# Giving two chains of small steps top priority, and moving the end's gradient and stores to other engines, in a decode backward kernel

## The chip, the core and the metric

The kernel runs on one core of a Trainium2 chip. The time is device microseconds of one launch. Thirteen runs of the kernel before gave a median of 498.91 us, from 496.43 to 502.22. The execution that was profiled took 496.43 us, and its span (first to last instruction) is 494.7 us.

## The reference

The forward pass is one decode step of a layer with two branches that run beside each other, for two sequences and one new token each. `D` is 576, there are 32 query heads on 16 key and value heads of 128, 4096 cached keys per head, and a gated layer of width 4608:

```
xn  = layernorm(x)
q   = xn @ wq                        # 32 heads of 128
p   = softmax(q k^T / sqrt(128))     # over 4096 cached keys, two query heads share a kv head
out = x + (p v) @ wo + ((xn @ w_gate) * (xn @ w_up)) @ w_down
```

What is computed is `out` and the gradient of all eight inputs for a given `grad_out`: `x`, the two caches, `wq`, `wo`, `w_gate`, `w_up`, `w_down`. Everything is bf16. The gradients of the caches are outer products (probabilities times output gradient for V, score gradients times queries for K), each as large as the cache: 92 MB are read, 92 MB written.

## The kernel before, in words

**Steps.** The 16 key and value heads are taken in 4 groups of 4. A group has 4 steps (2 sequences, and 2 heads at a time), so there are 16 steps (the loop over `n`, L887). A step loads two K heads and two V heads, 1 MB each, into a pool of 12 buffers (tag `nat`). VectorE (DVE) transposes each half head (`X`, L547, L141), and TensorE (PE) makes the scores of it (`ps_sc`, L556).

**The softmax chain** (`softmax`, L623) follows when both K heads of the step have scores. It is a row of small instructions that hand over from engine to engine: DVE copies the scores (`s_sb`, L565), PE transposes them (L569), DVE takes row maxima (`mx`, L626), PE transposes these (L628), DVE takes the maxima of 4 (`m4`, L630), PE spreads them (L632), DVE makes the bias (`negb`, L635), ScalarE (ACT) takes the exponential and its sum (`ex`, L641), PE adds the sums (L643), DVE inverts (`rz`, L645), scales (`pr`, L648) and transposes (`rowT`). **The score gradient chain** (`dscores`, L657) does the like after the V heads: L565, L569, L661, L666, L668, L669 and a transpose. Its first product needs `ex`, so it stands behind the softmax chain of the same step.

**What hangs on the chains.** GpSimd (POOL) spreads each result under a mask (`prm` and `dsm`, L597). Each of the two then feeds 8 outer product units (`outer_units`, L601): two PE matmuls of 512 columns into `ps_o`, and one eviction of 128x1024 to a store tile `so` by ACT (L124). After four units POOL issues a store of 1 MB (L618). The rows also go into `contract` (L572): 64 small matmuls with the V or K heads, which is the last use of these heads, so their buffers come free only then, and SP can issue the next loads.

**Side work.** The gated layer and the end of each group (`back_units`: output projection, gradients of `wq` and `wo`) are cut into units, which the loop mixes in (`side`, L779). They evict with ACT too.

**The end.** After the loop (L930) the list `ending` is filled. From there `evac` (L116) deals the evictions out to ACT and DVE by a running sum of costs, and every third pair of outputs goes to the banks of the scores (`ps_x`). The remaining units are mixed with the units of the last gradient, in this order: `prepare`, the first two units of the last group, `output`, `rows`, `gradient` (L854), then the stores of the last `wo` and `wq` gradients: `outer_o` (tile `sto`, L764), `outer_q` (`stq`, L730) and `outer_qt` (`stqt`, L745), all issued by POOL. `gradient` works on 2x576 numbers: two reductions on DVE (L858, L862), then five DVE instructions (L867, L869, L870, L871, L873) and a store by SP (L874).

**What sets the order.** Each engine takes its instructions strictly in its queue's order. The orders are fixed when the kernel is built: the framework walks through its own model of the run and gives an engine, among the instructions whose inputs the model holds ready, the one that stands first in the program. Inside `tc.high_priority()` an instruction counts as standing ahead of all others. `Block` (L95) has always used this for groups of matmuls that belong together. SP's queue holds all loads, POOL's queue holds the stores as well as POOL's arithmetic.

Of the kernel before, what the change touches and what calls it, by code (L numbers as in the profile page):

```python
# [9 lines left out]
ALU = mybir.AluOpType  # L10
# [3 lines left out]
P = 128  # L14


def view(t, p0, np_, off, dims):

    (pstep, _), *_ = t.ap
    return bass.AP(t.tensor, t.offset + p0 * pstep + off, [[pstep, np_], *[list(d) for d in dims]])  # L20
# [3 lines left out]
def kernel(  # L24
# [22 lines left out]
    nc = tc.nc  # L47
# [8 lines left out]
    GH = 2 * G  # L56
    NGRP = Hkv // G
# [16 lines left out]
    def ps_m(shape, dtype=FP32):  # L74
        return ps.tile(list(shape), dtype, tag="m", bufs=2, name="ps_m")
# [4 lines left out]
    def ps_o():  # L80
        return ps.tile([P, 2, 512], FP32, tag="o", bufs=2, name="ps_o")
# [52 lines left out]
    def dve(us):  # L134
        load["v"] += us
# [59 lines left out]
    xn_f = sb.tile([2, D], FP32, tag="nat", bufs=12, name="xn_f")  # L195
# [6 lines left out]
    rstd = const.tile([2, 1], FP32, name="rstd")  # L202
# [74 lines left out]
    def tailtile(name):  # L277
        return sb.tile([P, FS], BF16, tag="stt", bufs=2, name=name)
# [399 lines left out]
    def back_units(st):  # L678
        g, wq, wo, oT = st["g"], st["wq"], st["wo"], st["oT"]
        n0 = g * GH * Dh  # L680
        m = {}
        stq = nat if g == NGRP - 1 else swtile

        def first():
            yp = ps_m([P, 5, 2])
            with Block() as mm:
                for dc in range(5):
                    for h in range(GH):
                        mm(yp[:, dc, :], lhsT=wo[:, h, DOFF[dc]:DOFF[dc] + P], rhs=oT[:, 0, h, 0:2],
                                         start=(h == 0), stop=(h == GH - 1))  # L690
            nc.vector.tensor_add(acc[:], acc[:], yp[:])

            rp = ps_m([P, 2, 2, P], BF16)
            for t in range(2):
                for h in range(GH):
                    a = h // 2
                    nc.tensor.transpose(rp[32 * a:32 * a + 32, t, h % 2, :], oT[:, t, h, :], ident[:])
            m["R"] = R = sb.tile([P, 2, 2, P], BF16, tag="R", bufs=1, name="R")
            nc.vector.tensor_copy(R[:], rp[:])
            rp = ps_m([P, 32, 2])  # L700
            for be in range(4):
                nc.tensor.matmul(view(rp[:], 0, P, 2 * be, [[8, 8], [1, 2]]),
                                 lhsT=sel[:, be].rearrange("p a i -> p (a i)"), rhs=oT[:, 1, :, 0:2],
                                 start=True, stop=True)
            m["W"] = stationaries(rp[:], lambda h: (P * h, [[1, P]]))
            dve(0.2 + 0.5)

        def second():
            dxn(*m["W"], wq, lambda q, s: (s // 4) * 16 + q * 4 + s % 4, lambda s: s // 4, 2)

        def outer_q(k, A):
            def f():
                R = m["R"]
                if A == 0:
                    m["st"] = stq([P, 2, GH * P], "stq")
                st = m["st"]
                o, whole = ps_pair()
                with Block() as mm:
                    for dc in range(2):
                        for aa in range(2):  # L720
                            a = 2 * A + aa
                            d0 = (2 * k + dc) * P
                            mm(o[aa][:, 256 * dc:256 * dc + 256], lhsT=xnr[32 * a:32 * a + 32, d0:d0 + P],
                                             rhs=R[32 * a:32 * a + 32, 1].rearrange("p h d -> p (h d)"),
                                             start=True, stop=True)
                evac_pair(lambda aa: view(st[:], 0, P, 512 * A + 256 * (aa or 0),
                                          ([[256, 2]] if aa is None else []) + [[GH * P, 2], [1, 256]]), o, whole, 1024,
                          lambda x: x.rearrange("p a (d n) -> p a d n" if whole is not None else "p (d n) -> p d n", d=2))
                if A == 1:
                    nc.gpsimd.dma_start(out_4[256 * k:256 * k + 256, n0:n0 + GH * P].rearrange("(c p) n -> p c n", p=P),  # L730
                                        st[:])
            return f

        def outer_qt():
            R = m["R"]
            st = tailtile("stqt")
            for A in range(2):
                o = ps_o()
                with Block() as mm:
                    for aa in range(2):  # L740
                        a = 2 * A + aa
                        mm(o[64 * A:64 * A + 64, aa, 0:256], lhsT=xnr[32 * a:32 * a + 32, 512:576],
                                         rhs=R[32 * a:32 * a + 32, 1].rearrange("p h d -> p (h d)"), start=True, stop=True)
                evac(st[64 * A:64 * A + 64].rearrange("p (a n) -> p a n", a=2), o[64 * A:64 * A + 64, :, 0:256], 512)
                nc.gpsimd.dma_start(out_4[512:576, n0 + 512 * A:n0 + 512 * A + 512], st[64 * A:64 * A + 64])  # L745

        def outer_o(A, h2, k):
            def f():
                R = m["R"]
                if h2 == 0 and k == 0:  # L750
                    m["so"] = stq([P, 4, D], "sto")
                o, whole = ps_pair()
                with Block() as mm:
                    for aa in range(2):
                        a = 2 * A + aa
                        mm(o[aa][:, 0:HD2], lhsT=R[32 * a:32 * a + 32, 0, h2, :],
                                         rhs=dyr[32 * a:32 * a + 32, k * HD2:(k + 1) * HD2], start=True, stop=True)
                so = m["so"]
                evac_pair(lambda aa: view(so[:], 0, P, h2 * D + k * HD2 + 2 * D * (aa or 0),
                                          ([[2 * D, 2]] if aa is None else []) + [[1, HD2]]), o, whole, D,  # L760
                          lambda x: x[:, :, 0:HD2] if whole is not None else x[:, 0:HD2])
                if h2 == 1 and k == 1:
                    r0 = n0 + 4 * A * P
                    nc.gpsimd.dma_start(out_5[r0:r0 + 4 * P, :].rearrange("(h p) n -> p h n", p=P), m["so"][:])  # L764
            return f

        return [[first], [second], [outer_o(0, 0, 0), outer_o(0, 0, 1)], [outer_o(0, 1, 0), outer_o(0, 1, 1)],
                [outer_o(1, 0, 0), outer_o(1, 0, 1)], [outer_o(1, 1, 0), outer_o(1, 1, 1)],
                [outer_q(0, 0), outer_q(0, 1)], [outer_q(1, 0), outer_q(1, 1)], [outer_qt]]
# [43 lines left out]
    def final_units():  # L813
        m = {}
# [39 lines left out]
        def gradient():  # L854
            rowf, xn_f, dy_f = m["rowf"], m["xn"], m["dy"]
            dxn = rowf[:, 1, :]
            m1 = fin([2, 1], FP32, "m1")
            nc.vector.reduce_sum(m1[:], dxn, axis=AX.X)  # L858
            nc.vector.tensor_scalar(m1[:], m1[:], 1.0 / D, None, op0=ALU.mult)
            xs2 = fin([2, D], FP32, "xs2")  # L860
            m2 = fin([2, 1], FP32, "m2")
            nc.vector.tensor_tensor_reduce(  # L862
                out=xs2[:], in0=dxn, in1=xn_f[:], scale=1.0 / D, scalar=0.0,
                op0=ALU.mult, op1=ALU.add, accum_out=m2[:],
            )
            t1 = fin([2, D], FP32, "t1")
            nc.vector.tensor_scalar(t1[:], dxn, m1[:], None, op0=ALU.subtract)  # L867
            t3 = fin([2, D], FP32, "t3")
            nc.vector.tensor_scalar(t3[:], xn_f[:], m2[:], None, op0=ALU.mult)  # L869
            nc.vector.tensor_sub(t1[:], t1[:], t3[:])  # L870
            nc.vector.tensor_scalar(t1[:], t1[:], rstd[:], None, op0=ALU.mult)  # L871
            dx_bf = fin([2, D], BF16, "dx_bf")
            nc.vector.tensor_add(dx_bf[:], t1[:], dy_f[:])  # L873
            nc.sync.dma_start(out_1.rearrange("b s d -> (b s) d"), dx_bf[:])  # L874

        return [[prepare], [output], [rows], [gradient]]
# [6 lines left out]
    st = group_front(0, *loaded)  # L883
# [3 lines left out]
    for n in range(NIT):  # L887
        g, b, s = step(n)
# [7 lines left out]
        s_ps = ps_sc()  # L896
        for x in range(2):
            K.append(slot(kview, 0, b, l0 + x, s_ps, per, (lambda: end_of_K(*last[:5])) if x == 0 and last else None))
            if x == 0:
# [3 lines left out]
                        side[0:0] = back_units(last[0])  # L903
                        per = -(-len(side) // 4)
                bd1 = build_bd(st, b, s, 1)
        pr, pT, ex, rz = softmax(s_ps)
        prm = masked(pr, "prm")
        if n + 1 < NIT and not new:
            build_W(st, *step(n + 1)[1:], 0)
        dp_ps = ps_sc()  # L910
# [9 lines left out]
                    build_W(nxt, 0, 0, 0)  # L920
        if n + 1 < NIT:
            build_W(nxt if new else st, *step(n + 1)[1:], 1)
        ds, dsT = dscores(pr, ex, rz, dp_ps)
        dsm = masked(ds, "dsm")
        end_of_V(st, b, s, V, pT)
        last = (st, b, s, K, dsT, dsm, bd0)
        if new:
            st = nxt
# [40 lines left out]
```

## Time and profile before

| what | value |
|---|---|
| median of 13 runs (lowest, highest) | 498.91 us (496.43, 502.22) |
| profiled execution: its time, its span | 496.43 us, 494.7 us |
| busy: PE, PEld, DVE, ACT, POOL | 390.9, 259.2, 327.6, 348.4, 264.2 us |
| moved by DMA | 186.06 MB, 376 GB/s over the span |
| 0 to 440 us: DMA share, GB/s | 1.00, 392 |
| 440 to 494.7 us: DMA share, GB/s | 0.68, 248 |

Busy time is that of an engine's own instructions; issuing a DMA counts as busy on POOL only, where it takes 0.75 to 0.8 us for a store of 1 MB. The DMA share is the mean busy share of the core's 16 DMA engines; at 1 and 400 GB/s or more they have nothing left. The last load of a head is issued at 416.57 us and lands at 432.60; from then on only stores are left. In the timeline each row has a start, a duration, the engine, the line, what is written and read, and in brackets how long the engine had been idle and for whom it had waited.

### The profile page before, as it was taken

To read this page: it belongs to the slowest core of one execution; us is meant where nothing else is said; L and a number is where in the kernel's file an instruction comes from. 1 tells how busy PE (TensorE), PEld (TensorE's weight loads), DVE (VectorE), ACT (ScalarE), POOL (GpSimd) and SP (SyncE) were. 2 spreads that over 40 slices of the span, in tenths; PEclk is the share of its full clock that TensorE was granted. 3 is DMA by queue.
4 is the path that set the end of the run, shared out by engine and by line. 5 is a ranking of instruction groups with operands and counts; after the bars stand their busy time and mean duration, and the time that the engine had idled before them with its cause. 6 is when DMAs were issued, how large, how long until landed. Compare 5 with 4: busy or idle time off the path is not lost.

```text
span 494.7 us, 17062 instructions
## 1 busy us (share of the span) xinstructions
PE 390.9 (79%) x7417; PEld 259.2 (52%) x7417; DVE 327.6 (66%) x680; ACT 348.4 (70%) x439; POOL 264.2 (53%) x404
## 2 busy tenths in 40 slices
PE   2677979877878876889998778669888969898943
PEld 1565656654645554556665446446556537564510
DVE  6786794862839674955887475566777564984383
ACT  4143867768647957868986678748886767899833
POOL 3245456663635555576546346547647336587613
PEclk9965998899969989988999789969999798999995
DMA  7998999999999999999999999989999999996665
GB/s 250 384 399 317 354 415 399 422 419 408 339 393 362 411 416 366 419 414 411 402 419 406 418 418 347 416 366 369 407 422 408 416 422 363 414 383 239 261 260 191
DMA packets 52900, 186.06 MB, mean 376 GB/s; under 512 B 4141, under 2 KB 19129, under 8 KB 44633
## 3 DMA queue, kind: packets, MB, share of 16 engines
q1 hardware_dynamic: 28392, 92.49, 48.6%
q0 software_dynamic: 24432, 92.48, 47.2%
q8 instruction: 58, 0.95, 0.7%
q14 instruction: 18, 0.14, 0.1%
HBM read 92.48 MB, written 92.48 MB: 374 GB/s over the span
## 4 chain that ended last, share of the span: by engine, by line
PE 30%; DMA 28%; ACT 13%; DVE 9%; issue 9%; POOL 5%; POOLq 0%; ACTq 0%; DVEq 0%
DMA out_dram<-so 20%; PE ps_o L105 14%; ACT so L124 10%; PE ps_m L105 8%; PE ps_sc L105 5%; DMA kv<-in_A_k_cache_dram 4%; DVE X L141 4%; DMA out_dram<-stw 4%; POOL bd L532 2%; ACT std L124 1%; POOL prm L597 1%; DVE Xw L141 1%; PE ps_m L591 1%; POOL out_dram L764 1%; ACT stw L124 1%
## 5 line engine op out<-in xcount | busy, mean ns | idle before, releaser
L124 ACT CAST so<-ps_o 128x1024 bf16<-128x1024 f32 x249 | 238.6, 1022 | 68.8 <-PE ps_o L105 52.8
L141 DVE STREAM_TRANSPOSE X<-kv 128x1024 f32<-128x1024 f32 x128 | 157.3, 1232 | 34.1 <-PE ps_sc L105 14.1
L105 PEld LDWEIGHTS <-X 128*128 128x128 bf16 x2048 | 81.8, 103 | 32.3 <-DVE X L141 15.5
L105 PE MATMUL ps_sc<-W,X 128*128 128x64 bf16 (+1 forms) x2048 | 90.4, 200 | 6.2 <-DVE X L141 5.2
L618 POOL DMA_DIRECT2D out_dram<-so x64 | 50.0, 782 | 72.1 <-ACT so L124 47.5
L105 PE MATMUL ps_o<-bd,prm 128*128 128x512 bf16 x254 | 78.5, 412 | 11.5 <-ACT so L124 5.0
L105 PE MATMUL ps_o<-bd,dsm 128*128 128x512 bf16 x250 | 80.0, 411 | 8.6 <-ACT so L124 7.1
L532 POOL TENSOR_TENSOR bd<-dense,maskq 128x1024 bf16<-128x1024 bf16 x32 | 60.6, 1892 | 12.9 <-DVE dense L529 11.6
L124 ACT CAST stw<-ps_o 128x1024 bf16<-128x1024 f32 x36 | 34.4, 1020 | 16.2 <-PE ps_o L105 9.3
L124 ACT CAST std<-ps_o 128x576 bf16<-128x576 f32 x36 | 21.1, 649 | 29.0 <-PE ps_o L105 21.5
L105 PE MATMUL ps_m<-kv,rowT 128*32 128x128 bf16 x2048 | 38.1, 230 | 4.2 <-issue 4.0
L514 POOL COPY W<-rep 32x16 bf16<-32x16 bf16 x128 | 25.0, 195 | 26.7 <-PE ps_sc L105 18.9
L105 PEld LDWEIGHTS <-prm 128*128 128x128 bf16 x256 | 21.8, 104 | 30.5 <-issue 17.7
L597 POOL TENSOR_TENSOR prm<-pr,maskc 128x1024 bf16<-128x1024 bf16 x16 | 30.2, 1889 | 13.7 <-DVE pr L648 13.0
L105 PEld LDWEIGHTS <-dsm 128*128 128x128 bf16 x256 | 22.1, 104 | 27.8 <-issue 20.5
L105 PEld LDWEIGHTS <-rowT 128*32 128x32 bf16 x2048 | 31.8, 102 | 9.0 <-issue 7.0
L597 POOL TENSOR_TENSOR dsm<-ds,maskc 128x1024 bf16<-128x1024 bf16 x16 | 30.4, 1900 | 5.8 <-DVE ds L669 5.5
L124 ACT CAST sto<-ps_o 128x576 bf16<-128x576 f32 x27 | 16.4, 650 | 14.1 <-PE ps_o L105 12.8
L141 DVE STREAM_TRANSPOSE Xw<-wgu 128x1152 f32<-128x1152 f32 x18 | 24.2, 1354 | 2.2 <-PE ps_sc L105 2.2
L105 PEld LDWEIGHTS <-Wdy 128*128 128x128 bf16 x306 | 21.0, 104 | 7.8 <-DVE Xo L141 2.9
L414 POOL DMA_DIRECT2D out_dram<-stw x18 | 13.9, 770 | 18.0 <-ACT stw L124 18.0
L105 PEld LDWEIGHTS <-xnr 32*128 32x128 bf16 (+1 forms) x440 | 12.8, 97 | 20.0 <-issue 15.5
(186 smaller groups left out, 552.2 us busy)
## 6 DMA issues: line engine op xcount, KB each, us to landing
out_dram<-so POOLq DMA_DIRECT2D x64, 1024.0 KB, 12.8
kv<-in_A_k_cache_dram SPq DMA_DIRECT2D x32, 1024.0 KB, 13.0
kv<-in_A_v_cache_dram SPq DMA_DIRECT2D x32, 1024.0 KB, 15.6
out_dram<-stw POOLq DMA_DIRECT2D x18, 512.0 KB, 11.8
wd<-in_B_w_down_dram SPq DMA_DIRECT2D x9, 576.0 KB, 7.6
out_dram<-std POOLq DMA_DIRECT2D x9, 576.0 KB, 9.7
wo<-in_A_wo_dram SPq DMA_DIRECT2D x4, 1152.0 KB, 12.7
wgu<-in_B_w_gate_dram SPq DMA_DIRECT2D x9, 512.0 KB, 14.2
```

The source lines that it names most:

```text
L105: ins = nc.tensor.matmul(*args, **kwargs)
L124: nc.scalar.copy(out, in_)
L141: nc.vector.transpose(out, in_)
L414: nc.gpsimd.dma_start(out[0:512, f0:f0 + FS].rearrange("(c p) n -> p c n", p=P), st[:])
L514: nc.gpsimd.tensor_copy(view(W[t][:], 32 * a, 32, 48 + 4 * a, [[2 * WW, 4], [WW + 2, 2], [1, 2]]), view(st["rep"][:], 32 * a, 32, t * 4 * ...
L532: nc.gpsimd.tensor_tensor(bd[:], view(dense[:], 0, P, 0, [[Dh, 2], [0, 4], [1, Dh]]), view(maskq[:], 0, P, 0, [[0, 2], [1, 4], [0, Dh]]), ...
L591: nc.tensor.matmul(t_ps[:], lhsT=o_sb[:], rhs=RV[:].rearrange("p x r -> p (x r)"), start=True, stop=True)
L597: nc.gpsimd.tensor_tensor(m[:], view(rows[:], 0, P, 0, [[0, 8], [1, P]]), view(maskc[:], 0, P, 0, [[1, 8], [0, P]]), ALU.mult)
L618: nc.gpsimd.dma_start(oview[b, :, :, l0 + x].rearrange("a m n -> m a n"), st[:].rearrange("p a c d -> p a (c d)"))
L764: nc.gpsimd.dma_start(out_5[r0:r0 + 4 * P, :].rearrange("(h p) n -> p h n", p=P), m["so"][:])
```

## The change

Three edits:

- `softmax` and `dscores` are traced inside `tc.high_priority()`, on every engine they use (DVE, PE, ACT). The mask products `prm` and `dsm`, the contractions and the outer products are not.
- In the last group alone (`g == NGRP - 1`) the stores of `sto`, `stq` and `stqt` are issued by SP in place of POOL.
- In `gradient` the five DVE instructions become four on POOL: both `tensor_scalar` take `rstd` as a second operand, so that the separate multiplication (L871) goes. The two reductions stay on DVE.

```
+        store = nc.sync.dma_start if g == NGRP - 1 else nc.gpsimd.dma_start
...
-                    nc.gpsimd.dma_start(out_4[256 * k:256 * k + 256, n0:n0 + GH * P].rearrange("(c p) n -> p c n", p=P),
+                    store(out_4[256 * k:256 * k + 256, n0:n0 + GH * P].rearrange("(c p) n -> p c n", p=P),
...
-                nc.gpsimd.dma_start(out_4[512:576, n0 + 512 * A:n0 + 512 * A + 512], st[64 * A:64 * A + 64])
+                store(out_4[512:576, n0 + 512 * A:n0 + 512 * A + 512], st[64 * A:64 * A + 64])
...
-                    nc.gpsimd.dma_start(out_5[r0:r0 + 4 * P, :].rearrange("(h p) n -> p h n", p=P), m["so"][:])
+                    store(out_5[r0:r0 + 4 * P, :].rearrange("(h p) n -> p h n", p=P), m["so"][:])
...
-            nc.vector.tensor_scalar(t1[:], dxn, m1[:], None, op0=ALU.subtract)
+            nc.gpsimd.tensor_scalar(t1[:], dxn, m1[:], rstd[:], op0=ALU.subtract, op1=ALU.mult)
             t3 = fin([2, D], FP32, "t3")
-            nc.vector.tensor_scalar(t3[:], xn_f[:], m2[:], None, op0=ALU.mult)
-            nc.vector.tensor_sub(t1[:], t1[:], t3[:])
-            nc.vector.tensor_scalar(t1[:], t1[:], rstd[:], None, op0=ALU.mult)
+            nc.gpsimd.tensor_scalar(t3[:], xn_f[:], m2[:], rstd[:], op0=ALU.mult, op1=ALU.mult)
+            nc.gpsimd.tensor_sub(t1[:], t1[:], t3[:])
             dx_bf = fin([2, D], BF16, "dx_bf")
-            nc.vector.tensor_add(dx_bf[:], t1[:], dy_f[:])
+            nc.gpsimd.tensor_add(dx_bf[:], t1[:], dy_f[:])
...
-        pr, pT, ex, rz = softmax(s_ps)
+        with tc.high_priority():
+            pr, pT, ex, rz = softmax(s_ps)
...
-        ds, dsT = dscores(pr, ex, rz, dp_ps)
+        with tc.high_priority():
+            ds, dsT = dscores(pr, ex, rz, dp_ps)
```

## The prediction

> **What bounds the kernel now.** I read the page first, its DMA row above all: 40 slices, a digit for the busy tenths of the 16 DMA engines.
>
> ```profile
> DMA  7998999999999999999999999989999999996665
> ```
>
> From the second slice to the 36th the DMA engines are full, so in the middle an engine that is earlier gains little; what is to be had is idle DMA time. In windows of 5 us it adds up to about 9 us before 440 us (the first load 2.7, then 45 to 55, 130 to 135, 295 to 305 and 330 to 335 us) and about 18 us after 440, where only stores are left: 13.55 MB, which at the 400 GB/s of the full stretches are 34 us of the 54.7. So the end is where I look next, cut at the places where the timeline changes character. Columns: stretch, length, busy us (count) of PE, PEld, DVE, ACT, POOL, PE clock, DMA share, GB/s.
>
> ```profile
> 448.00:455.50 7.50, 5.43 (x35) 2.27 (x36) 1.79 (x5) 7.46 (x9) 4.98 (x6) 1.00 0.60 205
> 455.50:463.50 8.00, 7.29 (x181) 4.82 (x181) 4.00 (x15) 6.91 (x9) 7.02 (x5) 1.00 0.65 247
> 463.50:473.00 9.50, 8.48 (x113) 3.61 (x111) 4.96 (x9) 8.53 (x12) 2.93 (x6) 1.00 0.85 321
> 473.00:476.10 3.10, 2.36 (x13) 0.82 (x13) 2.20 (x8) 0.00 (x0) 0.00 (x0) 1.00 0.97 361
> 478.30:481.30 3.00, 0.00 (x0) 0.00 (x0) 2.86 (x6) 0.00 (x0) 0.00 (x0) 0.97 0.85 321
> 481.30:487.70 6.40, 4.30 (x27) 1.21 (x26) 5.04 (x9) 4.13 (x6) 3.03 (x5) 0.50 0.54 191
> ```
>
> ACT evicts without a gap from 448 to 455.5, nearly so to 473, and then stands still for 3.10 us and later for 3.00 us, the second time together with PE and POOL. The end is bound by evictions first, then by the chain of the last gradient, which passes through DVE and PE ahead of the evictions queued behind it.
>
> **The priority, in the last step.** The timeline around the last softmax:
>
> ```profile
> 448.04 7.43 ACT L124 CAST so<-ps_o 128x1024 bf16<-128x1024 f32 x8 [0.24 <-PE ps_o L105]
> 448.39 0.08 DVE L635 DVE_READ_ACCUMULATOR2_ANT negb<- 128x1 f32 x1
> 455.32 0.42 ACT L641 ACTIVATE ex<-ps_sc,negb 128x128 f32<-128x128 f32 x1
> 455.85 0.29 DVE L661 CUSTOM_DVE_ANT_0 ds<-ex,ps_sc 128x128 bf16<-128x128 f32 x1 [5.91 <-ACT ex L641]
> ```
>
> The exponential's bias is there at 448.5, but it stands in ACT's queue behind eight evictions and starts at 455.3; DVE waits 5.91 us for it. At top priority it goes after the eviction that is running (7.43 / 8 = 0.93 us each), so by 449.5, and all that hangs on it comes 5 to 6 us earlier: `pr`, `prm`, both `contract` calls, the last group's units and the gradient. No work is saved on ACT (0.65 us of exponential only change places with evictions), so the gain is ACT's idle time alone. In 455.5 to 463.5 ACT is idle 1.1 us (waiting for the first `prm` units), in 463.5 to 473 it is 1.0, and in 473 to 476.1 it is 3.10: there PE waits with the `rows` matmuls (L845) for `accx`, and the evictions' matmuls stand behind them in PE's queue. With that chain 5 us earlier `accx` is there before PE asks. Bounds: nothing, if POOL's stores keep the gradient back anyway (the second `Wt` copy, L292 at 470.04, waits 2.5 us behind a store), and 5.2 us, if all three go. I take the 3.1 and a little of the rest: **3.5 us**.
>
> **The priority, in the middle.** One step shows how the order hurts there:
>
> ```profile
> 316.39 0.24 DVE L630 TENSOR_REDUCE m<-ps_m 1x4 f32<-1x128 f32 x1
> ...
> 323.82 1.25 DVE L141 STREAM_TRANSPOSE X<-kv 128x1024 f32<-128x1024 f32 x1 [7.19 <-DMA kv<-in_A_k_cache_dram]
> 324.99 0.12 DVE L635 CUSTOM_DVE_ANT_0 nb<-ps_m,R 128x4 f32<-128x4 f32 x1
> ...
> 326.25 0.64 ACT L124 CAST std<-ps_o 128x576 bf16<-128x576 f32 x1 [7.04 <-PE ps_o L105]
> ```
>
> `negb` stands behind a transpose that waits 7.19 us for a load; meanwhile ACT starves for 7.04 us. From the copy of the scores (309.7) to `pr` (329.2) this chain takes 19.5 us, in the step at 390.9 it takes 18.8, in the quickest (337.7 to 343.2) 5.5. The contractions that free the heads' buffers hang on it: the last K loads are issued at 414.08 after `pr` at 409.7. So loads are issued earlier and idle spots such as 130 to 135 and 330 to 335 us (shares 0.79 and 0.69, about 1.0 and 1.6 us lost) may fill. But the DMA engines are full elsewhere, and the first load's 2.7 us stay. Gain between nothing and some 5 us; as most spots follow loads of the gated layer too, I take **1 us**. What it may cost is the third rival.
>
> **The gradient off DVE.** Five DVE rows go, of which first, last and the store that waited:
>
> ```profile
> 478.36 0.51 DVE L867 TENSOR_SCALAR t<-rowf,m 2x576 f32<-2x576 f32 x1
> ...
> 480.65 0.75 DVE L873 TENSOR_TENSOR dx_bf<-t,dy_f 2x576 bf16<-2x576 f32 x1
> ...
> 482.99 0.75 POOL L764 DMA_DIRECT2D out_dram<-sto  x1 [4.75 <-DVE sto L121]
> ```
>
> Their durations are 0.51 + 0.50 + 0.75 + 0.51 + 0.75 = 3.0 us, 478.36 to 481.4, and this is the stretch in which PE, ACT and POOL do nothing at all: DVE's evictions of `sto` (L121, 481.33) are next in its queue, PE waits for their banks, ACT for PE, the store for all. Bounds: nothing, and 4.4 us (PE's whole wait); I take **3.0 us**, since what follows is the same work 3.0 us earlier.
>
> On POOL four instructions come in. POOL has done such work once, and the mask product is the nearest with two inputs:
>
> ```profile
> 448.04 2.30 POOL L826 TENSOR_SCALAR xn_f<-x_f,mu,rstd 2x576 f32<-2x576 f32 x1
> ```
>
> Two `tensor_scalar` at 2.30 make 4.6 us. For the sum and the difference no row has this shape: the mask product (L597) takes 1.9 us for 1024 columns of two bf16 inputs, so 1.07 us for 576 by columns; the bounds are the one-input cast of this size (0.66, L822) and the 2.30. So 4.6 + 2 x 1.07 = 6.7 us, between 5.9 and 9.2: more than twice what DVE needed. What hides it: in before `m2` is ready at 478.2, with the chain earlier by 3.5 us at 474.7, so POOL ends near 481.5, and `dx_bf` is stored while `sto` and `stq` are still evicted and 2.3 MB of them still to be moved. Without that cover POOL ends at 478.2 + 6.7 to 9.2, so 485 to 487.4, which is still before the last store was issued in before (488.15), but not before it will be now.
>
> The Trainium skill speaks against this edit: GPSIMD Engine Reference, section 4.1 Engine selection, sends elementwise work to VectorE and calls GpSimd about 2 times slower with two inputs and roughly equal with one. The row above has it worse: 2.30 us against 0.51 on DVE for one tensor input, 4.5 times. An estimate by that page would be 1.0 us for the two `tensor_scalar` and 3.0 for the other two, 4 us in all; the prediction goes by the row.
>
> **The stores by SP.** POOL's six last issues take 0.75, 0.75, 1.42 for two and 1.11 for two; the last begins at 488.15, after the last eviction ended at 487.62. With SP they need not stand behind POOL's 6.7 us, which is what this edit is for. SP's loads of 576 KB (L337) take 0.34 us to issue. Behind the last eviction one issue is left in place of two: **0.5 us**. How long a store through SP's queue takes to land no row shows; POOL's of this size took 3.5 to 5.0 us, SP's load of 576 KB 5.0 at the least. I take no difference, and keep from 0.5 less to 1.5 more. SP's queue is empty by then but for two small stores, of which `dx_bf` waits for POOL: the second rival.
>
> **Sum.** 3.5 + 1 + 3.0 + 0.5 = 8 us off the profiled execution's 496.43, so 488.4. The profiled execution is 2.5 us under the median of the runs shown, so I set the same 8 us against 498.91: **491 us**. The full DMA does not forbid it: 13.55 MB fit into the 46.7 us that are left from 440 at 290 GB/s.
>
> **Rivals.**
>
> *The priority changes nothing that counts.* The model behind the queues may have held the exponential ready only where it stands now, or POOL's stores keep the gradient back. Against it: the bias was ready 6.8 us before, beside eight evictions that need nothing else. Then 3.5 us are left from the other edits: 495.4.
>
> *SP's queue blocks.* If `dx_bf`'s store stands ahead of the `sto` and `stq` stores, it holds 2.3 MB until POOL is through, at 485 to 487.4 if the chain came no earlier. Then come 2.3 MB at 400 GB/s, 5.8 us, and the 2.4 us from the last landing (492.28) to the end: 493 to 495.6 against 494.7. No change, some 498. It happens if the builder thinks POOL quicker than it is.
>
> *Slower: the exponential holds ACT.* A queue cannot be left: if `ex` is put ahead of evictions that are ready, and its bias comes later on the chip than in the model, ACT waits. The quickest chain has 4.0 us from `s_sb` to `ex` (337.7 to 341.7), seven changes of engine. In the middle ACT can bear it (27.9 of 40 us busy from 380 to 420). From 400 on it can't: 25.5 of 28 us busy from 420 to 448, then as above. The exponentials at 407.3, 434.5 and 455.3 fall there; 3 x 4 = 12 us, less the 3.5 of the other edits, gives 8.5 us more: 507. It decides from about 2.7 us of waiting per exponential (3 x 2.7 = 8, all that I count on).
>
> **Chances.** Forecast 0.50 (its own range 485 to 495), priority without effect 0.16, SP blocks 0.12, ACT held 0.22. A measurement of this kernel tells some 0.5% (2.5 us) from no change. The first two are faster by more, together 0.66; the third is within it, 0.12; the last is slower, 0.22. The range goes from 484 (5.2 for the last step, 5 for the middle, 4.4 for the gradient would be 484) to 504, which takes in the lighter half of the slower case.
>
> **What would show it.** Right: the last `ex` within 1.5 us of its `negb`; no wait near 6 us at L661; the time from `s_sb` to `pr` near 6 us in most steps; no stretch in which PE, ACT and POOL are all still at the end; four POOL rows of 1 to 2.3 us with evictions beside them; the span's last 55 us moving 13 MB at 280 GB/s or more. Wrong: ACT idle "<- DVE negb" for microseconds after 400 us (it has 2.9 us in 3 places now); SP waiting for POOL's `dx_bf` with stores behind it; DMA shares below 0.9 at new places in the middle.

## The result, and the profile after

The changed kernel takes **506.68 us** in the median (503.57 to 512.19, 11 runs), the kernel before 499.0 beside it: a ratio of 1.0156, 95% interval 1.0128 to 1.0183. (A run more than 1.5% above the fastest of the same kernel is left out of the ratios, here and below, but not out of the medians, so the two need not agree exactly.) Forecast were 491 us and a range up to 504. The change makes the kernel slower. The profiled execution took 506.54 us with a span of 504.7, so 10.0 us of span have to be found. For lines 683 to 870 of before the changed kernel's line numbers are one above; L873 and L874 are the same in both.

The DMA row of the page of after, in the same 40 slices:

```profile
DMA  7997999999999999999999999999999999747685
```

The middle is as full as it was: one slice below 9 between the second and the 34th, where before had two. The end is worse: the DMA engines are full up to the 34th slice only, where they were up to the 36th, and the 36th (442 to 454 us) is at 4. Next the windows of both kernels, in the columns of the prediction's table; first before, then after.

```profile
0.00:420.00 420.00, 337.42 (x6524) 229.21 (x6525) 280.47 (x582) 293.96 (x368) 224.72 (x354) 0.90 1.00 391
420.00:440.00 20.00, 17.39 (x349) 11.54 (x350) 17.75 (x36) 18.27 (x25) 12.36 (x22) 1.00 1.02 412
440.00:460.00 20.00, 17.43 (x312) 10.21 (x315) 10.47 (x26) 18.54 (x24) 15.93 (x16) 1.00 0.78 281
```

```profile
0.00:420.00 420.00, 342.50 (x6522) 231.99 (x6522) 285.37 (x584) 290.10 (x363) 223.25 (x352) 0.89 1.00 390
420.00:440.00 20.00, 15.61 (x203) 9.08 (x204) 10.40 (x20) 13.46 (x17) 6.50 (x17) 0.74 0.82 322
440.00:460.00 20.00, 18.23 (x349) 12.36 (x348) 14.70 (x34) 16.90 (x26) 17.09 (x15) 0.91 0.64 231
460.00:480.00 20.00, 16.46 (x285) 8.45 (x284) 6.04 (x19) 17.66 (x20) 11.13 (x13) 1.00 0.66 241
```

Read the fourth busy column, ACT. Up to 420 us after has done 3.9 us less of evictions, from 420 to 440 another 4.8, from 440 to 460 another 1.6: 10.3 us. The first reduction of the last gradient starts 10.2 us later (487.04 for 476.85). So the loss shows before 460, and nearly half of it between 420 and 440, where every engine does less than before and the DMA moves 322 GB/s where it moved 412 (20 us times 90 GB/s are 1.8 MB, or 4.5 us at 400 GB/s). The timeline shows what stands still there:

```profile
422.19 0.25 DVE L626 TENSOR_REDUCE mx<-ps_sc 128x1 f32<-128x128 f32 x1
...
427.58 2.84 ACT L124 CAST so<-ps_o 128x1024 bf16<-128x1024 f32 x3 [4.45 <-DMA out_dram<-so]
428.65 0.59 PE L105 MATMUL ps_o<-bd,prm 128*128 128x512 bf16 x2 [2.90 <-ACT so L124]
...
431.46 1.25 DVE L141 STREAM_TRANSPOSE X<-kv 128x1024 f32<-128x1024 f32 x1 [4.43 <-PE ps_sc L105]
...
439.64 0.27 PE L628 MATMUL ps_m<-identf,mx 128*1 128x128 f32 x1
...
441.73 0.39 ACT L641 ACTIVATE ex<-ps_sc,negb 128x128 f32<-128x128 f32 x1
```

Each bracket names the next link: ACT has no free `so` buffer until an earlier store has landed, PE's outer products wait for ACT, the scores behind them in PE's queue wait too, and DVE waits for the scores. The maxima `mx` of step 14 are ready at 422.4 but transposed at 439.64, and the whole softmax chain of this step takes 22.6 us, where it took 11.2 in before.

The last softmax, by contrast, goes as the edit wanted:

```profile
457.25 0.07 DVE L635 DVE_READ_ACCUMULATOR2_ANT negb<- 128x1 f32 x1
...
458.36 0.37 ACT L641 ACTIVATE ex<-ps_sc,negb 128x128 f32<-128x128 f32 x1
```

1.0 us from bias to exponential, where it was 6.9; but the bias itself comes at 457.25 for 448.39. Then the end, first the reduction and the last eviction of before, then after:

```profile
476.85 0.73 DVE L858 TENSOR_REDUCE m<-rowf 2x1 f32<-2x576 f32 x1
...
487.04 0.58 ACT L124 CAST stqt<-ps_o 64x512 bf16<-64x512 f32 x1 [0.51 <-PE ps_o L105]
```

```profile
487.04 0.73 DVE L859 TENSOR_REDUCE m<-rowf 2x1 f32<-2x576 f32 x1
...
488.62 2.29 POOL L868 TENSOR_SCALAR t<-rowf,m,rstd 2x576 f32<-2x576 f32 x1 [0.20 <-DVE m L860]
490.90 0.82 POOL L870 TENSOR_SCALAR t<-xn_f,m,rstd 2x576 f32<-2x576 f32 x1
491.80 1.39 POOL L871 TENSOR_TENSOR t<-t,t 2x576 f32<-2x576 f32 x1
493.27 1.39 POOL L873 TENSOR_TENSOR dx_bf<-t,dy_f 2x576 bf16<-2x576 f32 x1
494.19 0.58 ACT L124 CAST stqt<-ps_o 64x512 bf16<-64x512 f32 x1 [0.51 <-PE ps_o L105]
494.68 0.25 SPq L874 DMA_DIRECT2D out_dram<-dx_bf  x1
495.03 0.95 SPq L765 DMA_DIRECT2D out_dram<-sto  x2
...
498.57 2.65 SPq L746 DMA_DIRECT2D out_dram<-stqt  x2
```

From the reduction to the last eviction it is 7.7 us, before 10.8: 3.1 less, since the evictions no longer stand behind the gradient. From the last eviction to the end it is 9.9 us, before 7.0: 2.9 more. SP stands 10.8 us at the store of `dx_bf`, and six stores, some of whose tiles were complete at 491.6, are issued behind it from 495.03 on. So 10.2 - 3.1 + 2.9 = 10.0 us, the whole difference of the spans.

### The profile page after: what moved, and what is told of

Same layout as the page of the kernel before. It is cut to its first block, busy times and chain, and to the rows that moved or that the text cites. A ratio compares the mean times of both kernels' runs of the same rounds, so it can differ in the third digit from the quotient of the medians.

```text
span 504.7 us, 17053 instructions
## 1 busy us (share of the span) xinstructions
PE 401.8 (80%) x7417; PEld 265.5 (53%) x7417; DVE 328.4 (65%) x675; ACT 349.0 (69%) x439; POOL 266.1 (53%) x402
## 4 chain that ended last, share of the span: by engine, by line
PE 38%; DMA 24%; DVE 13%; ACT 10%; issue 6%; POOL 3%; ACTq 0%; DVEq 0%; POOLq 0%
PE ps_o L105 16%; DMA out_dram<-so 13%; PE ps_m L105 11%; ACT so L124 8%; PE ps_sc L105 7%; DVE X L141 6%; DMA kv<-in_A_k_cache_dram 6%; DMA kv<-in_A_v_cache_dram 5%; DVE Xw L141 2%; POOL bd L532 1%; PE ps_m L591 1%; DVE pr L648 1%; PE ps_m L643 1%; POOL prm L597 1%; PE ps_sc L569 1%
## 5 line engine op out<-in xcount | busy, mean ns | idle before, releaser
L105 PE MATMUL ps_sc<-W,X 128*128 128x64 bf16 (+1 forms) x2048 | 98.2, 205 | 11.5 <-DVE X L141 5.8
L105 PEld LDWEIGHTS <-X 128*128 128x128 bf16 x2048 | 88.7, 106 | 35.3 <-DVE X L141 15.2
L105 PE MATMUL ps_o<-bd,prm 128*128 128x512 bf16 x254 | 83.5, 432 | 14.3 <-ACT so L124 7.0
L105 PE MATMUL ps_o<-bd,dsm 128*128 128x512 bf16 x250 | 76.5, 403 | 7.3 <-ACT so L124 6.1
L532 POOL TENSOR_TENSOR bd<-dense,maskq 128x1024 bf16<-128x1024 bf16 x32 | 60.7, 1896 | 17.1 <-DVE dense L529 14.8
L597 POOL TENSOR_TENSOR dsm<-ds,maskc 128x1024 bf16<-128x1024 bf16 x16 | 30.3, 1895 | 5.2 <-DVE ds L669 5.0
L105 PEld LDWEIGHTS <-Wdy 128*128 128x128 bf16 x306 | 22.8, 111 | 9.3 <-issue 4.4
L521 POOL COPY dM<-qd 128x128 bf16<-128x128 bf16 x32 | 9.1, 289 | 31.5 <-PE ps_m L527 16.3
## 6 DMA issues: line engine op xcount, KB each, us to landing
kv<-in_A_v_cache_dram SPq DMA_DIRECT2D x32, 1024.0 KB, 17.1
```

The lines of the kernel that those rows point to most:

```text
L105: ins = nc.tensor.matmul(*args, **kwargs)
L521: nc.gpsimd.tensor_copy(view(dM[:], 0, P, t * 2 * P, [[P + 2, 2], [4, 32], [1, 2]]), view(st["qd"][:], 0, P, (2 if t == 0 else 1) * GH * 2 ...
L532: nc.gpsimd.tensor_tensor(bd[:], view(dense[:], 0, P, 0, [[Dh, 2], [0, 4], [1, Dh]]), view(maskq[:], 0, P, 0, [[0, 2], [1, 4], [0, Dh]]), ...
L597: nc.gpsimd.tensor_tensor(m[:], view(rows[:], 0, P, 0, [[0, 8], [1, P]]), view(maskc[:], 0, P, 0, [[1, 8], [0, P]]), ALU.mult)
```

## The experiments

Each ratio is against runs of the kernel before on the same chip, with a 95% interval; two runs within about 0.5% aren't told apart. Where an expectation shortens the theories: A, the priority carries the loss and the two edits at the end nearly cancel; M, the chains are held because their small outputs share few PSUM banks (`ps_m`) with other work; N or D, loads run ahead of stores, so that ACT has more left once the loads are done; F, the loss is made by the order of steps 13 and 14. The rivals of A at the outset were the gradient on POOL, and ACT held by the exponential.

### The parts of the change, one by one

`e1_prio` is the kernel before with the two `with tc.high_priority():` only; `e2_tail` has the other two edits only; `e3_tail_dxpool` is `e2_tail` with one line changed:

```
-            nc.sync.dma_start(out_1.rearrange("b s d -> (b s) d"), dx_bf[:])
+            nc.gpsimd.dma_start(out_1.rearrange("b s d -> (b s) d"), dx_bf[:])
```

> Priority on both chains alone; the gradient stays on DVE and all stores on POOL. Theory A (the loss is the priority's: in the changed kernel the reduction of the last gradient starts 10.2 us later than before, and only what follows it is shorter): about 9 to 11 us over the kernel before, 508 to 510, with the reduction (L858) starting near 487 us. Theory B (the two edits at the end lose the time, and the priority is neutral or better, as forecast): 494 to 499. Theory C (each edit reorders the whole schedule, and none has an effect of its own): anything, without relation to the reduction's start in the changed kernel.

> The two edits at the end without the priority: gradient on GpSimd, last group's stores by SP behind the store of dx. Theory A: from the reduction to the last eviction 7.7 us in place of 10.8 (3.1 gained), from the last eviction to the end 9.9 in place of 7.0 (2.9 lost, the six stores standing behind dx on SP): 498 to 500, no change. Theory B: 505 or more. The forecast's own step (stores by SP cost nothing) would give 495 to 496.

> As the run before, but the store of dx is issued by GpSimd itself, so that SP's queue holds nothing ahead of the last group's stores that waits for GpSimd. Theory A: the 2.9 us behind the last eviction go, the 3.1 stay gained: 495 to 496.5, with the sto stores issued within 1 us of their evictions. If SP's stores are slow for another reason (their issue or their landing), it stays at 498 to 500 although they no longer wait for dx.

Measured: `e1_prio` 508.5 us, 1.0147 (1.0102 to 1.0191), as much as the whole change. `e2_tail` 500.21, 1.0005 (0.9962 to 1.0049): nothing. `e3_tail_dxpool` 494.0, 0.9847 (0.9766 to 0.9929): faster than both kernels. So the priority carries the loss, the two edits at the end together are a gain, and the place of one small store in SP's queue takes that gain back. (No run has the gradient on POOL without the stores on SP.) In `e2_tail` SP issues `dx_bf` at 488.62 and the six stores from 488.97 on; in `e3_tail_dxpool` `sto` and `stq` go at 483.42 and 486.49, before `dx_bf` is there.

The same line in the changed kernel itself (`e18_after_dxpool`):

> The changed kernel with one edit: the store of dx_bf is issued by GpSimd, so that no store on SP's queue stands behind it. If the 2.9 us between the last eviction and the end come from the stores queued behind dx_bf, as e2 against e3 said (6 us by the medians), the time falls to 501 to 504 us, and the gap from the last eviction to the end goes from 9.9 us back to about 7. If the last 10 us are bound by the landing of the stores whatever queue they are on, it stays at 506 to 507.

504.39 us, 1.0123 (1.0075 to 1.0171). The end of its timeline:

```profile
492.15 1.55 SPq L765 DMA_DIRECT2D out_dram<-sto  x2
...
494.97 1.39 POOL L873 TENSOR_TENSOR dx_bf<-t,dy_f 2x576 bf16<-2x576 f32 x1
...
495.88 0.58 ACT L124 CAST stqt<-ps_o 64x512 bf16<-64x512 f32 x1 [0.51 <-PE ps_o L105]
496.43 2.56 SPq L746 DMA_DIRECT2D out_dram<-stqt  x2
496.65 0.60 POOL L874 DMA_DIRECT2D out_dram<-dx_bf  x1 [0.29 <-POOL dx_bf L873]
```

The `sto` stores go 2.8 us before `dx_bf` is even begun, and from the last eviction (496.5) to the end (502.7) it is 6.2 us in place of 9.9. The profile shows the term; the medians differ by 2.3 us, slightly less than expected, and the intervals overlap.

### Which of the two chains

`e4_prio_softmax` has the priority on `softmax` alone, `e8_prio_ds` on `dscores` alone.

> Priority on the softmax chain alone, nothing else changed. If the loss comes from the softmax chain (its exponential put into ACT's queue, its three small products that need the two shared banks of tag m): 505 or more, like both together. If it comes from the score gradient chain, which takes the shared banks and DVE while the next step's scores wait: 497 to 500. If it is the order as a whole (theory C): no relation to the run with both.

> Priority on the score gradient chain alone. Priority on the softmax chain alone took 507.6, both 508.5. If the softmax chain carries the loss: 498 to 502. If either does harm by itself and they share it: 504 or more.

`e4_prio_softmax` 507.61 us, 1.0104 (1.0015 to 1.0192); `e8_prio_ds` 502.77, 1.0049 (1.0016 to 1.0082). The softmax chain costs something, and more by the medians; `e8_prio_ds` is at the edge of what can be told, and lies between its two expectations.

### Is the chain too long

In `e1_prio` and after, the mean wait from scores to maxima falls from 2.9 to 1.4 us and from bias to exponential from 2.0 to 0.5 (0.65 in after), but from `mx` to `m4`, two instructions through a `ps_m` bank, it rises from 3.9 to 6.2 (6.3 in after): all in all 12.2 us (12.1) where it was 12.5. Three kernels give the small outputs of the chains a place in the bank of the transposed scores:

```
-        s_ps = ps_sc()
+        wide = ps.tile([P, 512], FP32, tag="sc", bufs=2, name="ps_row")
...
-        mT = ps_m([1, P])
+        s_ps, mT = wide[:, 0:P], wide[0:1, P:2 * P]
...
-        nb_ps = ps_m([P, 4])
-        z_ps = ps_m([P, 1])
+        nb_ps, z_ps = wide[:, 256:260], wide[:, 260:261]
...
-        c_ps = ps_m([P, 1])
+        dp_ps, c_ps = wide[:, 0:P], wide[:, 260:261]
```

`e5_prio_bank` does this to `e1_prio`, `e6_bank` to the kernel before, `e7_tail_dxpool_bank` to `e3_tail_dxpool`.

> Priority on both chains, and their four small PSUM outputs (the transposed maxima, the spread bias, the two sums) put into the bank that already holds the transposed scores, so that they need none of the two shared banks of tag m. Theory M (the priority only moves the wait: from the copy and the exponential, 2.9 and 2.1 us on average, to the step from mx to m4, 3.9 to 6.3, where the chain stands for a bank of tag m): mx to m4 falls under 2.5 us on average, the chain from s_sb to pr from 12 to 8 us or less, and the loss goes: 499 or less. Theory N (the loss has nothing to do with the banks, but with ACT standing behind full store buffers after 420 us): the chain may get shorter, the time stays at 506 or more.

> The same four outputs in the bank of the scores, without any priority. Theory M: mx to m4 falls here too, less time than before, 492 to 498. If the banks matter only together with the priority: 498 to 501.

> The end with the gradient on GpSimd, the last group's stores by SP and the store of dx by GpSimd (494.0 by itself), together with the four outputs in the bank of the scores, no priority. If the gains add: 5 to 6 us below the kernel with the banks alone, and below 494 if that one is faster than the kernel before. If they share one cover: 493 to 496.

In `e5_prio_bank` the wait is gone (1.1 us) and the chain takes 6.4 us on the mean, half of before. Its step 14, copy of the scores and `pr`, and a window behind it:

```profile
416.06 0.29 DVE L565 COPY s_sb<-ps_sc 128x128 f32<-128x128 f32 x1 [0.74 <-PE ps_sc L105]
...
420.84 0.33 DVE L647 TENSOR_SCALAR pr<-ex,rz 128x128 bf16<-128x128 f32 x1
```

```profile
430.00:440.00 10.00, 8.61 (x214) 5.85 (x213) 9.34 (x20) 8.22 (x11) 7.25 (x11) 1.00 0.54 192
```

4.8 us where after took 22.6, and still the DMA runs empty behind it (192 GB/s). The time is 504.84 us, 1.0116 (1.0065 to 1.0166). `e6_bank` is 503.46, 1.0063 (1.0036 to 1.009), and `e7_tail_dxpool_bank` 500.91, 1.0025 (0.9982 to 1.0068), 6.9 us above `e3_tail_dxpool` by the medians, though on another chip. So M falls as the cause of the loss: it was right on what holds the chain, but the chain's length is not what costs. The banks alone, which shorten the wait from `mx` to `m4` from 3.9 to 2.5 us and leave the chain at 12 us, make the kernel slower without any priority, as the priority does. The two costs don't add up: beside its own control `e6_bank`, on the same chip, the priority in `e5_prio_bank` costs 1.4 us by the medians, which can't be told from nothing.

### Where in the kernel

The priority only in the last step (`e13_prio_last`), only up to step 12 (`e14_prio_first13`), only in steps 13 and 14 (`e15_prio_13_14`), on both chains:

```
+        with tc.high_priority() if n == NIT - 1 else ExitStack():
             pr, pT, ex, rz = softmax(s_ps)
```

> Priority on the two chains of the last step alone (n = 15). Theory F (the loss arises in one place, in the two steps before the last, where loads that come sooner and full store buffers hold ACT, PE behind it, and the chain behind PE; the last chain itself gains what was forecast): the last exponential starts within 1.5 us of its bias (455.3 before, so about 450), and the time is 2 to 4 us under the kernel before. Theory G (the priority harms wherever it stands, since what it puts ahead on one engine holds the others): 500 or more.

> Priority on the chains of the first 13 steps alone (n up to 12), where the DMA engines are full. Theory F, as far as the last steps' order makes the loss: 497 to 501. If it is the loads' getting ahead of the stores, which these steps bring about, that makes it: 505 or more, although the steps with the stall have no priority.

> Priority on the chains of the two steps before the last alone (n = 13 and 14). Theory F, order of these steps: 505 or more, with the copy of the last step's K scores at 450 us or later. If the first 13 steps bring the loss about: 497 to 501, with that copy near 444.

`e13_prio_last` 497.92 us, 1.0003 (0.9973 to 1.0033). Its last chain, and its last eviction:

```profile
450.00 0.07 DVE L635 DVE_READ_ACCUMULATOR2_ANT negb<- 128x1 f32 x1
...
451.24 0.37 ACT L641 ACTIVATE ex<-ps_sc,negb 128x128 f32<-128x128 f32 x1
...
488.07 0.58 ACT L124 CAST stqt<-ps_o 64x512 bf16<-64x512 f32 x1 [0.51 <-PE ps_o L105]
```

The exponential follows its bias at once, `pr` comes at 452.9 for 456.8, and the last eviction still ends at 488.65 (before 487.6). The 3.9 us are lost again on the way to the end. That profile copies the last step's K scores 2.1 us later than before does (445.72 for 443.65), and the waits of ACT that were to go do shrink a little: between the exponential and the `sto` evictions they are 3.6 us (0.97, 1.36 and 1.29), where before had 5.2. `e15_prio_13_14` 500.17, 1.0023 (0.9987 to 1.0059): no loss that can be told, F falls. `e14_prio_first13` 502.92, 1.0111 (1.0051 to 1.0172): by the ratios most of the loss comes from the priority in the first 13 steps, though it lies between its two expectations and its interval just overlaps that of `e15_prio_13_14`.

### Is ACT the bound after the loads

Four kernels let DVE take evictions from step 14 on, where before waits for `ending`:

```
-        if ending and load["v"] + cv < load["s"] + cs:
+        if sharing and load["v"] + cv < load["s"] + cs:
...
+        if n == 14:
+            sharing.append(1)
+            load["v"] = load["s"] = 0.0
```

`e9_share` is this in the kernel before, `e10_prio_share` in `e1_prio`, `e12_taildx_share` in `e3_tail_dxpool`, and `e16_all_but_m` has this, the priority, the banks and the end of `e3_tail_dxpool`.

> Nothing of the change; DVE takes its part of the evictions from the 15th step on (n = 14, some 60 us earlier than the list called ending does it). It is the control of the next run. Theory D (after the last load has landed, ACT's evictions bind: 48.7 us of ACT work were left then in the kernel before, 60.3 in the changed one, because faster chains free the head buffers earlier, the loads go ahead of the stores in full DMA engines, and the evictions they push back have to be done at the end by ACT alone): ACT's work left at the end is shared, so 490 to 496. Theory E (the end is bound by the hand-overs of the last chains, not by ACT): 498 or more.

> Priority on both chains (508.5 by itself), with the evictions shared between ACT and DVE from the 15th step on. Theory D: the priority costs 8.5 us because ACT binds at the end, so with DVE's help the loss is gone: within 3 us of the control without priority, 489 to 498. Theory E: the loss of 6 to 9 us beside the control stays.

> The end with the gradient and the store of dx on GpSimd and the last group's stores on SP (494.0 by itself), no priority, evictions shared from the 15th step on. Theory D: the gain of sharing comes on top, since the end's gradient stood in DVE's queue and sharing takes work from ACT: 486 to 491. If DVE becomes the bound at the end: 492 or more.

> Everything together: priority on both chains, their four small outputs in the bank of the scores, evictions shared from the 15th step on, gradient and store of dx on GpSimd, last group's stores on SP. With the cleaner chain the copy of the last K scores stood at 444 us, but 59.5 us were left behind it, with ACT at 20.0 of 20 us busy: if that was ACT's bound, sharing frees it, 485 to 491. If GpSimd's queue holds the last dsm (468 us against 461 before), 495 or more.

`e9_share` 496.82 us, 0.995 (0.9921 to 0.9979). `e10_prio_share` 507.5, 1.0143 (1.0068 to 1.0217): with the priority the help brings nothing. `e12_taildx_share` **492.71**, 0.9875 (0.9796 to 0.9955), is the lowest time found, not to be told from `e3_tail_dxpool`. `e16_all_but_m` 504.4, 1.0134 (1.0075 to 1.0193). So that ACT has too much left to do is not the whole cause.

### Fewer load buffers

If loads run ahead of stores, a smaller pool for loads should hold them back: `nat` from 12 to 11 buffers, `st` from 5 to 6, with the priority (`e11_prio_bufs`) and without (`e17_bufs`).

> Priority on both chains, with 11 buffers of 1 MB for loads in place of 12, and 6 for stores of 1 MB in place of 5. Theory D: the loads can run ahead by one buffer less and the stores by one more, so that less of ACT's work is left when the last load lands (55 us or less in place of 62), and the loss shrinks to half or less: 499 to 504. Theory E: 507 or more, as fewer load buffers can only delay the chains.

> The kernel before with one load buffer fewer (nat 11) and one store buffer more (st 6), no priority: the control for e11_prio_bufs (522.5 us, ratio 1.045). If the loss of the priority comes from loads that run ahead of stores, the smaller load pool costs the kernel before something by itself, and e11's excess of 16 us over the priority alone is the pool's: this run is then 512 to 517 us. If the pool is harmless without the priority, it stays within 3 us of the kernel before, and e11's excess is an interplay of the two.

522.51 us, 1.0448 (1.0367 to 1.0528), and 515.85, 1.033 (1.0279 to 1.0382). The pool costs 17 us by itself, so `e11_prio_bufs` says nothing against N. But with this pool the priority still costs 522.51 / 515.85 = 1.013 by the medians (the two ran on different chips, and the intervals of their ratios overlap slightly), and there the last load lands later with it (460.6 for 453.7), not earlier. The time behind that landing is no longer (58.6 us for 59.9). This loss lies ahead of it, where the DMA engines are idle for 30.3 us in place of 22.5, added up in windows of 5 us. So if it is one, loads that are done early are not needed for a loss.

### What all runs have in common

| run | us | ratio | ACT busy 420 to 430 | DMA share, GB/s, 430 to 440 |
|---|---|---|---|---|
| before | 499.0 | 1 | 8.77 | 1.02, 406 |
| `e12_taildx_share` | 492.71 | 0.9875 | 7.71 | 1.02, 411 |
| `e3_tail_dxpool` | 494.0 | 0.9847 | 9.39 | 1.02, 414 |
| `e9_share` | 496.82 | 0.995 | 7.86 | 1.02, 414 |
| `e13_prio_last` | 497.92 | 1.0003 | 8.55 | 1.02, 411 |
| `e15_prio_13_14` | 500.17 | 1.0023 | 8.96 | 1.01, 403 |
| `e2_tail` | 500.21 | 1.0005 | 9.28 | 1.02, 412 |
| `e8_prio_ds` | 502.77 | 1.0049 | 9.36 | 1.02, 412 |
| `e14_prio_first13` | 502.92 | 1.0111 | 9.11 | 1.02, 414 |
| `e7_tail_dxpool_bank` | 500.91 | 1.0025 | 5.40 | 0.48, 169 |
| `e6_bank` | 503.46 | 1.0063 | 4.64 | 0.69, 267 |
| `e18_after_dxpool` | 504.39 | 1.0123 | 3.85 | 0.87, 325 |
| `e16_all_but_m` | 504.4 | 1.0134 | 6.12 | 0.58, 208 |
| `e5_prio_bank` | 504.84 | 1.0116 | 5.39 | 0.54, 192 |
| after | 506.68 | 1.0156 | 5.49 | 0.63, 228 |
| `e10_prio_share` | 507.5 | 1.0143 | 4.01 | 0.61, 221 |
| `e4_prio_softmax` | 507.61 | 1.0104 | 6.38 | 0.69, 249 |
| `e1_prio` | 508.5 | 1.0147 | 3.39 | 0.63, 231 |

The upper nine rows have no hole in the DMA from 430 to 440 us, the lower nine have one, with nothing between (`e18_after_dxpool` 0.87, with the rest of its hole behind 440). In the lower nine ACT is also busy for less than 6.5 of the 10 us from 420 to 430. These nine are the kernels that have the priority on the softmax chain in all steps, or the banks, or both; no other has the hole. (The two with the smaller pool aren't in the table, as their loads end 20 us and more later.)

The columns stand at fixed times, though, and the last load lands at 432.6 to 437.6 us in the upper nine and at 421.7 to 431.5 in the lower nine. So loads still fill a part of 430 to 440 above and hardly any of it below. In the 10 us behind each run's own last landing the DMA share is 0.79 to 1.01 above and 0.59 to 0.81 below: the groups overlap there (`e9_share` 0.79, `e10_prio_share` 0.81). What parts them cleanly is what is left when the loads are done. Above it is 37.5 to 44.8 us of work for ACT and 16.2 to 17.1 MB to move (before 43.2 and 16.6), below 50.6 to 57.2 us and 18.0 to 19.5 MB (after 54.3 and 18.3); and from there to the end it takes 57.1 to 64.6 us above, 71.2 to 80.2 below. In after the loads are done 3.5 us earlier than in before (429.1 for 432.6) and the rest takes 13.5 us longer (75.5 for 62.1): together the 10.0 us of the spans.

In the lower nine ACT waits for a store to land before it can evict, 3.0 to 9.6 us between 410 and 440. In the upper nine it is nothing to 2.3 us, but 4.2 in `e14_prio_first13`. `e14_prio_first13` is the exception that I can't place: its ratio shows a loss and its profiled execution no hole, but that execution was the fastest of its four (500.65 of 500.65 to 505.20).

**What stays open** is why chains that are served earlier bring the kernel to the end of its loads with more evictions and stores left. That this work is what makes the end late is read from the profiles; no run changes it alone, and giving a part of it to DVE (`e10_prio_share`) didn't help. What is seen is that at 420 us after has moved 90.5 MB of loads and 72.6 of stores, before 89.7 and 73.7, with the same sum. A store of 1 MB is four evictions of 1.02 us, so 1.1 MB are 4.5 us of ACT, beside the 3.9 that it lacks there. That the earlier chains free the heads' buffers earlier, and that SP's loads then take DMA time from the stores, fits this, but the runs with the smaller pool speak against it as the only cause, and no run here takes the one without the other.

## Why the prediction was wrong

**The bound.** Right that DMA bounds the middle and evictions the end. Wrong in what followed from it: "in the middle an engine that is earlier gains little" was taken to mean that it can't lose either. The slower kernels finish their loads earlier, with more evictions and stores left behind them. That an earlier chain, with the DMA full, changes which transfers come first fits this, but isn't shown by itself.

**The priority in the middle: the step that failed.** The prediction put it at 1 us gained, between nothing and 5. `e1_prio` measured 1.5% lost with nothing else changed, about 7 us of the paired runs, and 9.3 us of span in its profile (504.0 for 494.7). By the ratios `e14_prio_first13` puts most of it into the first 13 steps. The lower bound of nothing had no reason behind it but the full DMA, and a cost was priced only as ACT held by the exponential, in the third rival. What was to show it, "the time from `s_sb` to `pr` near 6 us in most steps", was wrong too, 12.1 us on the mean in after: a top place in the order doesn't help an instruction that waits for a bank which other work holds. And `e5_prio_bank`, which has the 6 us, is still slower than before (1.0116).

**The priority in the last step: 3.5 us, measured nothing.** `e13_prio_last` did to the chain just what was foreseen, 3.9 us earlier, and the ratio is 1.0003 (0.9973 to 1.0033). Of the 5.2 us of ACT's idle time that were to go by it some 1.5 went in its profile (3.1 to 1.3 us ahead of `sto`, with a new wait of 1.4 before); the prediction's own bound of nothing held here, for which `e13_prio_last` names no single cause.

**The gradient off DVE: 3.0 us, measured 3.1** (10.8 to 7.7 from the reduction to the last eviction). The four instructions on POOL take 5.9 us, the lower end of 5.9 to 9.2 where 6.7 was taken. The Trainium skill, GPSIMD Engine Reference, section 4.1 Engine selection, gives about twice VectorE's time for two inputs and calls one input roughly line-rate. The rows here have 1.39 us against 0.75 for two tensors, 1.9 times, which agrees, and 2.29 and 0.82 us against 0.51 and 0.50 for one tensor, which doesn't (though the form on POOL does two operations where DVE's did one). That this work is slower on POOL cost nothing by itself, because no eviction waits for it; what did wait for it was SP.

**The stores by SP: 0.5 us gained, measured 2.9 lost.** This is the rival "SP's queue blocks", given 0.12 and taken for a matter of its own. It came true by its mechanism: `dx_bf` stands ahead of the `sto` stores, "SP waiting for POOL's `dx_bf` with stores behind it" for 10.8 us. It eats the gradient's 3.1 us (`e2_tail` 1.0005 with it, `e3_tail_dxpool` 0.9847 without). The prediction's sentence that SP's queue is empty but for two small stores named the culprit and priced it in a rival only.

**The other rivals.** "The exponential holds ACT" gave 507 us, and 506.68 were measured, but by another way: in after ACT waits for `negb` for 3.3 us at one place in the whole execution and nowhere behind 400 us, where 12 us in three places were reckoned. The number agrees, the reason doesn't. "The priority changes nothing that counts" was wrong with it.

**The signs.** Seen as foretold: the last `ex` within 1.5 us, no long wait at L661, POOL rows of 0.8 to 2.3 us beside evictions. Missed: over the last 55 us 238 GB/s were moved, not 280. Of the signs of being wrong, SP's wait for `dx_bf` came, and a DMA share of 0.63 from 430 to 440 us. The sign that should have been asked for is how much ACT still has to evict when the last load has landed.

## What to carry to other kernels

When the DMA engines are full, a quicker chain need not be a gain, and can be a loss. Look how much is left to evict and to store at the moment when the last load lands (here 43.2 us of ACT before and 54.3 after), and how long the rest takes from there, before you count it as a gain. And before a store is put on a queue, list what stands behind it there. One store of 2 KB that waits for a slow engine kept six others back. Issuing it from the engine that makes its data cut the time from the last eviction to the end from 9.8 to 6.2 us (`e2_tail`, `e3_tail_dxpool`) and from 9.9 to 6.2 (after, `e18_after_dxpool`); the medians fell by 6.2 and 2.3 us.

## What the runs showed of the hardware

`tensor_scalar` on POOL, 2x576 with two operands of one number per partition, took 2.29 to 2.30 us where it subtracts and multiplies: `xn_f` in every profile, and the first instruction of the gradient. It took 0.82 us where it multiplies twice, the gradient's second instruction, in all seven profiles that have it on POOL. That second one also follows directly on another `tensor_scalar`; no run separates the operation from the place in the row. The last issues on SP are not cheap: two stores of `stqt`, 64 KB each, occupy it from 498.57 for 2.65 us, where POOL took 1.11 us for its two.
